# Attention and two gated layers on one core: the weights' conversion with a parametric ReLU on ACT and two DVE steps, and output weights in five fixed steps

## The chip, the core and the metric

The kernel runs on one core of a Trainium2 chip. Its engines work side by side: TensorE (PE) multiplies matrices, with its weight loads (PEld) beside it, VectorE (DVE), ScalarE (ACT) and GpSimd (POOL) do elementwise work, and SP issues transfers between HBM and the core's memory. The metric is the device time of one execution in microseconds; smaller is better. Three runs of the kernel before took 1116.43 to 1116.81 us, with a median of 1116.7 us.

## The reference, cut to what matters

```python
out1 = attention(q, k, v, mem_k, mem_v)      # 4 batches, 8 heads, 768 tokens in chunks of 32
x = out1 as (3072 tokens, 512)
x = ((x @ w1) * (x @ w2) @ w3) @ w_out       # moe:  512 -> 1024 -> 1024 -> 512, w3 @ w_out first
x = ((x @ w_a) * (x @ w_b)) @ w_out          # moe2: 512 -> 1536 -> 512
```

The weights (`moe_w1`, `moe_w2`, `moe_w3`, `moe_w_out`, `moe2_w_a`, `moe2_w_b`, `moe2_w_out`) come as 64-bit floating point numbers. [...]

## The kernel before

**Conversion of a block.** A block `raw` holds 512 or 1024 numbers per partition, each as a low word `l` and a high word `h`. `w_scale` (lines 372 to 379) runs on ACT: line 378 multiplies the high word, read as a 32-bit number, by a power of two, and line 379 does the like to the low word. `w_bits` (lines 381 to 385) runs on DVE: line 383 shifts the high word left by 3 and clears the sign bit, line 384 takes the sign bit out of `h` and sets it in the shifted word, and line 385 adds the low part. The names of the results are `w_f` (blocks of `w3` and the first `w_out`, 13 conversions) and `dec` (all others, 52).

**Stage 1, to about 95 us.** PE multiplies `w3` by `w_out` (`wps`), in two halves of 64 products. Between the products the attention of the first 14 or so units runs: scores `sc`, maximum `mx` (line 186 and 187), exponentials on ACT (line 209), the sum's reciprocal (lines 220 and 221), a multiplication on POOL (line 222), transposes `pt` and the product with the values `xp`. The order in which all this is issued is written out: `attn_slot` advances the attention by one slot, `w_tick` the conversions by one step. Four PSUM banks hold `wps`; `w_evict` empties them through ACT (line 570) and DVE (line 571), and the second half of the products takes the banks as they come free.

**Stage 2, to about 567 us.** For six tiles of 512 tokens `ab_step` forms `psA` and `psB` (w1 and w2), their product `gv` on DVE (line 635) with its two halves on ACT (636) and POOL (637), and `psY`. `between` stands after each half of a step and issues one `w_tick` while blocks of w1 and w2 remain, later one step of `c_weights` (the blocks of w_a and w_b), and the attention's slots for the next tile.

**Stage 3, to the end.** Three passes (`seq`) over pairs of token tiles; in each, twelve steps `f` of `seven`: 42 products `ps` in seven groups of six, with their sums on ACT (`copied`, line 830) and DVE (`plus`, line 835), and at the end `times` (lines 840 to 842 on DVE, ACT and POOL). Behind each step from the second on, 12 products `ops` with the output weights `fo` of the step before. In the first pass alone the output weights are converted as well: `w_out_blocks` is a generator with four steps for a block (scale on ACT; bits on DVE; upper half on ACT, line 143; lower half on DVE, line 146), and `other(n)` in `seven` runs `n` steps of it: two after the fifth group, one after the sixth, two at the end. With four steps for a block and five in a round of `seven`, the place of a block's step differs from round to round.

PE, DVE, ACT and POOL each work through their own queue in the order in which the program issues; an instruction that waits holds up all behind it on its engine.

Of the kernel before, what the change touches and what calls it, by code (L numbers as in the profile page):

```python
# [10 lines left out]
AF = mybir.ActivationFunctionType  # L11
ALU = mybir.AluOpType
# [31 lines left out]
def tile_attention_moe(  # L44
# [16 lines left out]
    nc = tc.nc  # L61
# [80 lines left out]
    def split_hi(hi, src):  # L142
        nc.scalar.activation(hi, src, AF.Copy)

    def split_lo(lo, src, hi):
        nc.vector.tensor_tensor(lo, src, hi.bitcast(F32), ALU.subtract)  # L146
# [225 lines left out]
    def w_scale(r):  # L372

        l, h = r[:, :, 0], r[:, :, 1].bitcast(F32)
        nc.scalar.activation(h, h, AF.Copy, scale=2.0**-112)  # L378
        nc.scalar.activation(l, l, AF.Copy, scale=2.0**-29)

    def w_bits(a, r):
        l, h = r[:, :, 0], r[:, :, 1]
        nc.vector.tensor_scalar(a, h, 3, 0x7FFFFFF8, ALU.logical_shift_left, ALU.bitwise_and)  # L383
        nc.vector.scalar_tensor_tensor(a, h, 0x80000000, a, ALU.bitwise_and, ALU.bitwise_or)  # L384
        nc.vector.tensor_tensor(a, a, l, ALU.add)  # L385

    def halves_of(i, *tiles):
# [52 lines left out]
    def w_new(pool, tag, n=None):  # L440
        return pool.tile([P, 2, CH], F32R, tag=tag, bufs=n, name=tag)
# [14 lines left out]
    def blocks_of(stage, src, out, bufs, raws_n=2):  # L456

        raws = []

        def load():  # L460
            if src:
                r = stage.tile([P, CH, 2], U32, tag="raw64", bufs=raws_n, name="raw64")
                nc.sync.dma_start(out=r.rearrange("p c w -> p (c w)"), in_=src.pop(0))
                raws.append(r)

        load()
        load()
        yield
        while raws:
            r = raws.pop(0)  # L470
            w_scale(r)
            yield
            a = stage.tile([P, CH], U32, tag="dec", bufs=bufs, name="dec")
            w_bits(a, r)
            load()
            out.append(a.bitcast(F32))
            yield
# [185 lines left out]
    def x_new():  # L663
        t = wpool.tile([P, 2, 2 * CH], F32R, tag="w12", name="x7")
        return t.rearrange("p l (k t) -> p l k t", k=2)
# [5 lines left out]
    def minus(x, y):  # L671
        z = tmp()
        nc.vector.tensor_tensor(z, x, y, ALU.subtract)
        return z

    def y_load(t, n):
        y = tmp()
        nc.sync.dma_start(out=y, in_=yd[t][:, n, :])
        return y

    def x_first(xs, k, t):
        b11, b21 = y_load(t, k), y_load(t, 2 + k)
        x_put(xs[0], k, b11)
        x_put(xs[1], k, b21)
        return b11, b21
# [12 lines left out]
    def w7_load(f):  # L698
        t = xpool.tile([P, 2, KD, TT], F32R, tag="xt", name="w7")
        t = t.rearrange("p l k t -> p (l k t)")[:, 0 : 7 * CH]  # L700
        src = wcd[f].rearrange("p i c -> p (i c)")
        for c0, c1 in ((0, 3 * CH), (3 * CH, 7 * CH)):
            nc.gpsimd.dma_start(out=t[:, c0:c1].bitcast(F32), in_=src[:, c0:c1])  # L703
        w7.append(t.rearrange("p (i l k f) -> p i l k f", i=7, l=2, k=2))

    w7 = []
# [87 lines left out]
    def w_out_blocks():  # L794
        blocks = []
        conv = blocks_of(stage2, [w2o[f] for f in range(M2)], blocks, 1)
        next(conv)
        yield
        for f in range(M2):
            for _ in range(2):  # L800
                next(conv)
                yield
            if f < 4:
                w = cp.tile([P, 2, CH], F32R, tag="fo", bufs=4, name="fo")
            else:
                w = w_new(wpool, "wo")
            x = blocks.pop()
            split_hi(w[:, 0, :], x)
            yield
            split_lo(w[:, 1, :], x, w[:, 0, :])  # L810
            fo.append(w)
            yield

    def product(ps, i, w, first):
        n = 0
        for k in range(2):
            for a, b in PASSES:
                nc.tensor.matmul(  # L818
                    ps,
                    lhsT=w[:, i, a, k, :],  # L820
                    rhs=xs[i][:, b, k, :],
                    start=first and n == 0,
                    stop=n == 5,
                    skip_group_check=not first,
                )
                n += 1

    def copied(ps):
        z = tmp()
        nc.scalar.activation(z, ps, AF.Copy)  # L830
        return z

    def plus(ps, y):
        z = tmp()
        nc.vector.tensor_tensor(z, ps, y, ALU.add)  # L835
        return z

    def times(x, y, g2):
        z = tmp()
        nc.vector.tensor_tensor(z, x, y, ALU.mult)  # L840
        nc.scalar.activation(g2[:, 0, :], z, AF.Copy)  # L841
        nc.gpsimd.tensor_tensor(g2[:, 1, :], z, g2[:, 0, :].bitcast(F32), ALU.subtract)  # L842

    def bank():
        return psd.tile([P, 512], F32, tag="d", name="ps7")[:, :TT]

    def seven(w, g1, g2, other, after):

        pa, pb = bank(), bank()
        product(pa, 0, w, True)  # L850
        s1 = copied(pa)
        next(late, None)
        product(pb, 1, w, True)
        c11 = plus(pb, s1)
        next(late, None)
        product(pa, 2, w, False)
        u2 = copied(pa)
        next(late, None)
        pc = bank()
        product(pc, 3, w, True)  # L860
        s5 = copied(pc)
        product(pa, 4, w, False)
        c22 = plus(pa, s5)
        other(2)
        product(pc, 5, w, False)
        c12 = plus(pc, u2)
        other(1)
        product(pa, 6, w, False)
        after()
        times(pa, c11, g1)  # L870
        times(c12, c22, g2)
        other(2)

    def out_part(ops, f, g2):
        for s in range(NS):
            for i, (a, b) in enumerate(PASSES):
                mm(
                    ops[s],
                    g2[:, a, P * s : P * s + P],
                    fo[f][:, b, :],  # L880
                    f == 0 and i == 0,
                    f == M2 - 1 and i == 2,
                )

    def out_new(pool, tag):
        return [pool.tile([P, 512], F32, tag=tag, name="ops") for _ in range(NS)]

    def out_store(ops, t):
        for s in range(NS):
            ob = tmp()  # L890
            if s % 2 == 0:
                nc.vector.tensor_copy(ob, ops[s])
            else:
                nc.scalar.activation(ob, ops[s], AF.Copy)
            r0 = t * TT + s * P
            nc.sync.dma_start(out=out[r0 : r0 + P, :], in_=ob)
# [6 lines left out]
    def other(n):  # L903
        for _ in range(n):
            next(cw, None)

    seq = [NT1 - 2] + list(range(0, NT1 - 2, 2))
    for si, t in enumerate(seq):
        nxt = seq[si + 1] if si + 1 < len(seq) else None
        g1, g2 = [], []  # L910
        spare = xs.pop().rearrange("p l k t -> p k l t")
        ops = out_new(pso, "o")
        for f in range(M2):
            g1.append(cp.tile([P, 2, TT], F32R, tag="g1", bufs=3, name="g1"))
            if f < M2 - 2:
                g2.append(cp.tile([P, 2, TT], F32R, tag="g2", bufs=M2 - 2, name="g2"))
            else:
                g2.append(spare[:, f - M2 + 2])

            def after():  # L920
                if f + 2 < M2 or nxt is not None:
                    w7_load((f + 2) % M2)

            seven(w7.pop(0), g1[f], g2[f], other, after)
            while len(fo) < f:
                next(cw)
            if f > 0:
                out_part(ops, f - 1, g1[f - 1])
        while len(fo) < M2:
            next(cw)  # L930
        ops2 = out_new(psd, "d")
        out_part(ops2, 0, g2[0])
        out_part(ops, M2 - 1, g1[M2 - 1])
        out_store(ops, t)
        if nxt is not None:
            xs = [x_new() for _ in range(8)]
            for k in range(2):
                b11, b21 = x_first(xs, k, nxt)
                b12, b22 = y_load(nxt + 1, k), y_load(nxt + 1, 2 + k)
                t1 = minus(b12, b11)  # L940
                x_put(xs[3], k, t1)
                for _ in x_rest(xs, k, b11, b21, b12, t1, b22):
                    pass
        for f in range(1, M2):
            out_part(ops2, f, g2[f])
        out_store(ops2, t + 1)
        if si == 0:
            stagestack.close()
# [83 lines left out]
```

## Time and profile before

| | |
|---|---|
| median of three runs | 1116.7 us |
| the profiled execution | 1116.64 us, span 1114.9 us |
| PE busy | 1094.1 us, 98% of the span |
| PEld busy | 874.9 us, 78% |
| DVE busy | 613.8 us, 55% |
| ACT busy | 516.3 us, 46% |
| POOL busy | 295.5 us, 27% |
| mean granted clock of TensorE | 0.998 |

The span runs from the first to the last instruction; 1.7 us of the execution lie outside it. PE is busy nearly throughout, so the time can only change where PE waits, or where its clock or the number of its instructions changes. The views that are read for that are the list of waits of PE, the groups by line, the order of time around each wait, and the busy time by stretches.

### The profile page before, as it was taken

To read this page: it belongs to the slowest core of one execution; us is meant where nothing else is said; L and a number is where in the kernel's file an instruction comes from. 1 tells how busy PE (TensorE), PEld (TensorE's weight loads), DVE (VectorE), ACT (ScalarE), POOL (GpSimd) and SP (SyncE) were. 2 spreads that over 40 slices of the span, in tenths; PEclk is the share of its full clock that TensorE was granted. 3 is DMA by queue.
4 is the path that set the end of the run, shared out by engine and by line. 5 is a ranking of instruction groups with operands and counts; after the bars stand their busy time and mean duration, and the time that the engine had idled before them with its cause. 6 is when DMAs were issued, how large, how long until landed. Compare 5 with 4: busy or idle time off the path is not lost.

```text
span 1114.9 us, 15510 instructions
## 1 busy us (share of the span) xinstructions
PE 1094.1 (98%) x5354; PEld 874.9 (78%) x5354; DVE 613.8 (55%) x1342; ACT 516.3 (46%) x1299; POOL 295.5 (27%) x308
## 2 busy tenths in 40 slices
PE   8899999999999999999999999999999999999998
PEld 3456888888878888888877878888888888888887
DVE  6879966876886777755766564252322243322220
ACT  6777656766766766745453343232222223222210
POOL 2452232321321322221212333202232211232210
PEclk9999999999999999999999999999999999999999
DMA  8845536345445444437545555424344352344311
GB/s 300 276 136 173 153 100 224 111 146 185 133 137 185 140 137 147 148 111 234 191 161 192 190 193 192 173 90 153 133 159 172 132 179 103 133 154 177 132 38 38
DMA packets 61671, 174.55 MB, mean 157 GB/s; under 512 B 8022, under 2 KB 18080, under 8 KB 55577
## 3 DMA queue, kind: packets, MB, share of 16 engines
q1 hardware_dynamic: 48762, 102.38, 27.7%
q0 software_dynamic: 12544, 70.91, 17.8%
q8 instruction: 42, 0.69, 0.3%
q14 instruction: 36, 0.29, 0.1%
q10 hardware_dynamic: 287, 0.27, 0.1%
HBM read 139.97 MB, written 33.55 MB: 156 GB/s over the span
## 4 chain that ended last, share of the span: by engine, by line
PE 85%; DVE 3%; ACT 2%; issue 1%; DMA 0%; DVEq 0%; ACTq 0%
PE ps L818 29%; PE ops L92 17%; PE psA L92 11%; PE psB L92 11%; PE psY L92 11%; PE sc L92 2%; PE xp L92 2%; PE pt L230 1%; DVE dec L384 1%; DVE dec L385 0%; ACT t L209 0%; DVE dec L383 0%; DMA wc<-co 0%; ACT raw L378 0%; DVE x L146 0%
## 5 line engine op out<-in xcount | busy, mean ns | idle before, releaser
L818 PE MATMUL ps<-x,w 128*128 128x512 f32 x1512 | 349.6, 390 | 3.8 <-ACT tmp L830 3.8
L818 PEld LDWEIGHTS ps<-x,w 128*128 128x128 f32 x1512 | 283.3, 188 | 64.7 <-ACT tmp L830 5.9
L835 DVE TENSOR_TENSOR tmp<-ps,tmp 128x512 f32<-128x512 f32 x108 | 74.6, 691 | 245.0 <-PE ps L818 240.9
L92 PE MATMUL psA<-xt,w 128*128 128x512 f32 x576 | 143.3, 398 | 0.0
L92 PE MATMUL psB<-xt,w 128*128 128x512 f32 x576 | 141.3, 394 | 0.0
L92 PE MATMUL psY<-g,wo 128*128 128x512 f32 x576 | 139.0, 393 | 0.0
L703 POOL DMA_DIRECT2D w<-wc x72 | 40.1, 559 | 368.9 <-PE ps L818 368.5
L830 ACT ACTIVATE tmp<-ps 128x512 f32<-128x512 f32 x108 | 64.6, 598 | 146.8 <-PE ps L818 133.9
L92 PEld LDWEIGHTS psA<-xt,w 128*128 128x128 f32 x576 | 106.8, 190 | 22.2 <-DVE dec L383 0.2
L92 PEld LDWEIGHTS psY<-g,wo 128*128 128x128 f32 x576 | 105.8, 188 | 21.3
L92 PEld LDWEIGHTS psB<-xt,w 128*128 128x128 f32 x576 | 105.5, 188 | 21.3
L222 POOL TENSOR_TENSOR t<-t,sm 96x512 f32<-96x512 f32 x64 | 67.7, 1058 | 196.3 <-DVE sm L221 107.9
L92 PE MATMUL ops<-wo,g 128*128 128x512 f32 x504 | 118.6, 389 | 0.0
L637 POOL TENSOR_TENSOR g<-gv,g 128x512 fp32r<-128x512 f32 x48 | 66.2, 1379 | 173.8 <-ACT g L636 173.6
L92 PEld LDWEIGHTS ops<-wo,g 128*128 128x128 f32 x504 | 94.6, 188 | 19.6
L841 ACT ACTIVATE g<-tmp 128x512 fp32r<-128x512 f32 x66 | 40.8, 635 | 130.4 <-DVE tmp L840 130.4
L842 POOL TENSOR_TENSOR g<-tmp,g 128x512 fp32r<-128x512 f32 x66 | 87.1, 1343 | 26.5 <-ACT g L841 26.0
L209 ACT ACTIVATE t<-t,mx 96x128 f32<-96x128 f32 x168 | 65.2, 393 | 7.8 <-DVE mx L194 7.8
L92 PE MATMUL ops<-fo,g 128*128 128x512 f32 x288 | 68.2, 389 | 0.0
L92 PE MATMUL wps<-w_f 128*128 128x512 f32 x128 | 59.7, 597 | 4.5 <-DVE w_f L385 2.6
L92 PEld LDWEIGHTS ops<-fo,g 128*128 128x128 f32 x288 | 54.1, 188 | 11.2
L636 ACT ACTIVATE g<-gv 128x512 fp32r<-128x512 f32 x48 | 30.3, 631 | 51.6 <-DVE gv L635 50.8
(83 smaller groups left out, 1293.7 us busy)
## 6 DMA issues: line engine op xcount, KB each, us to landing
w<-wc POOLq DMA_DIRECT2D x36, 1024.0 KB, 6.8
w<-wc POOLq DMA_DIRECT2D x36, 768.0 KB, 4.9
wc<-co SPq DMA_DIRECT2D x84, 256.0 KB, 2.5
raw<-in_wab SPq DMA_DIRECT2D x24, 512.0 KB, 4.0
kraw<-in_kt SPq DMA_DIRECT2D x42, 256.0 KB, 3.1
raw<-in_w SPq DMA_DIRECT2D x16, 512.0 KB, 3.8
raw<-in_w3a SPq DMA_DIRECT2D x7, 1024.0 KB, 9.0
vraw<-in_vw SPq DMA_DIRECT2D x50, 128.0 KB, 3.3
```

What stands on the lines that cost most here:

```text
L92: nc.tensor.matmul(o, lhsT=l, rhs=r, start=first, stop=last)
L209: nc.scalar.activation(t[:, h, :], src[:, h, :], AF.Exp, bias=mx[:, h : h + 1], scale=scale, accum_out=sm[:, h : h + 1],)
L222: nc.gpsimd.tensor_tensor(t, t, sm[:, :, None].to_broadcast([GQ, HH, KW]), ALU.mult)
L230: nc.tensor.transpose(pt[:, h, :], t[:, h, :], id_sb)
L636: nc.scalar.activation(g2[:, 0, :], gv, AF.Copy)
L637: nc.gpsimd.tensor_tensor(g2[:, 1, :], gv, g2[:, 0, :].bitcast(F32), ALU.subtract)
L703: nc.gpsimd.dma_start(out=t[:, c0:c1].bitcast(F32), in_=src[:, c0:c1])
L818: nc.tensor.matmul(ps, lhsT=w[:, i, a, k, :], rhs=xs[i][:, b, k, :], start=first and n == 0, stop=n == 5, skip_group_check=not first,)
L830: nc.scalar.activation(z, ps, AF.Copy)
L835: nc.vector.tensor_tensor(z, ps, y, ALU.add)
L841: nc.scalar.activation(g2[:, 0, :], z, AF.Copy)
L842: nc.gpsimd.tensor_tensor(g2[:, 1, :], z, g2[:, 0, :].bitcast(F32), ALU.subtract)
```

## The change

`w_scale` scales the high word with a parametric ReLU in place of a copy: positive numbers are multiplied by 2^-112 as before, negative ones by 2^-112 and by 2^32, which sets one more bit in the exponent field. `w_bits` shifts the word left by 3 with nothing cleared: the sign is shifted out, and that bit of the exponent comes to stand where the sign belongs. Line 384 is gone, and the low part is added as before.

`w_out_blocks` has a fifth step for each block, in which nothing is issued, so that a block takes exactly one round of `seven`. The two steps at the end of a round are moved ahead, to behind the sum of the second group, and are left out in the round f = 0.

```diff
         l, h = r[:, :, 0], r[:, :, 1].bitcast(F32)
-        nc.scalar.activation(h, h, AF.Copy, scale=2.0**-112)
+        nc.scalar.activation(h, h, AF.Prelu, scale=2.0**-112, alpha=2.0**32)
         nc.scalar.activation(l, l, AF.Copy, scale=2.0**-29)
 
     def w_bits(a, r):
         l, h = r[:, :, 0], r[:, :, 1]
-        nc.vector.tensor_scalar(a, h, 3, 0x7FFFFFF8, ALU.logical_shift_left, ALU.bitwise_and)
-        nc.vector.scalar_tensor_tensor(a, h, 0x80000000, a, ALU.bitwise_and, ALU.bitwise_or)
+        nc.vector.tensor_scalar(a, h, 3, None, ALU.logical_shift_left)
         nc.vector.tensor_tensor(a, a, l, ALU.add)
...
             for _ in range(2):
                 next(conv)
                 yield
+            yield
...
-    def seven(w, g1, g2, other, after):
+    def seven(w, g1, g2, other, after, lead):
...
         c11 = plus(pb, s1)
         next(late, None)
+        other(lead)
         product(pa, 2, w, False)
...
         times(c12, c22, g2)
-        other(2)
...
-            seven(w7.pop(0), g1[f], g2[f], other, after)
+            seven(w7.pop(0), g1[f], g2[f], other, after, 2 * (f > 0))
```

The order of PE, POOL and SP is the same in both kernels. DVE has 65 instructions fewer; ACT has the same number, in another order in the first pass of stage 3.

On DVE, at the conversion of a w1/w2 block early in stage 2 (`dec` is the block, `mx` the maximum of the scores, `gv` the product that the next matmuls are waiting for), before:

```order
L383 TENSOR_SCALAR dec<-raw_796 128x512
L384 SCALAR_TENSOR_TENSOR dec<-raw_796,dec 128x512
L385 ISA dec<-raw_796,dec 128x1024
L186 TENSOR_REDUCE mx<-sc 96x4
L187 TENSOR_SCALAR mx<-mx 96x4
L635 TENSOR_TENSOR gv<-psB,av 128x512
```

and after:

```order
L383 TENSOR_SCALAR dec<-raw_778 128x512
L384 ISA dec<-raw_778,dec 128x1024
L186 TENSOR_REDUCE mx<-sc 96x4
L187 TENSOR_SCALAR mx<-mx 96x4
L634 TENSOR_TENSOR gv<-psB,av 128x512
```

Between the shift and the add one instruction is gone, and `mx` and `gv` move up by one place; the same holds wherever a block is converted.

On ACT, in the first pass of stage 3, from the end of one round of `seven` into the next (L378 and L379 scale a block, L841 makes the upper halves of the round's two products, L143 `wo<-dec` is the upper half of a block of output weights, L830 copies a group's sum out of PSUM), before:

```order
L378 ACTIVATE raw_6525<-raw_6525 128x512
L379 ACTIVATE raw_6525<-raw_6525 128x512
L841 ACTIVATE g_6575<-tmp 128x512
L841 ACTIVATE g_6576<-tmp 128x512
L143 ACTIVATE wo<-dec 128x512
L830 ACTIVATE tmp<-ps_6672 128x512 x2
L830 ACTIVATE tmp<-ps_6698 128x512
```

and after:

```order
L378 ACTIVATE raw_6455<-raw_6455 128x512
L379 ACTIVATE raw_6455<-raw_6455 128x512
L841 ACTIVATE g_6586<-tmp 128x512
L841 ACTIVATE g_6587<-tmp 128x512
L830 ACTIVATE tmp<-ps_6680 128x512
L143 ACTIVATE wo<-dec 128x512
L830 ACTIVATE tmp<-ps_6680 128x512
L830 ACTIVATE tmp<-ps_6709 128x512
```

The upper half of a block now stands behind the first copy of a round in place of ahead of it, and it belongs to the block whose bits were made in the round before.

## Rows read from the trace of the kernel before

**Rows 1.** The page's first part: busy time, share of span, instructions.
```profile
PE 1094.1 (98%) x5354; PEld 874.9 (78%) x5354; DVE 613.8 (55%) x1342; ACT 516.3 (46%) x1299; POOL 295.5 (27%) x308
```

**Rows 2.** Waits of PE: who, for whom: us in total, times, longest us.
```profile
PE ps L818 <- ACT tmp L830: 3.8, 4, 1.5
PE wps L92 <- DVE w_f L385: 2.6, 2, 1.4
PE xp L92 <- ACT p L234: 2.2, 1, 2.2
PE wps L92 <- DVE wo L571: 1.9, 1, 1.9
PE sc L92 <- DVE mx L187: 1.8, 1, 1.8
...
PE sc L92 <- DVE q L146: 1.6, 2, 1.1
PE pt L230 <- ACT p L234: 0.6, 1, 0.6
PE sc L92 <- DVE w_f L383: 0.5, 1, 0.5
```

**Rows 3.** Groups by line, shapes apart: busy us, mean ns, idle before.
```profile
L384 DVE SCALAR_TENSOR_TENSOR dec<-raw,dec 128x512 uint32<-128x512 uint32 x52 | 45.8, 880 | 1.8
L209 ACT ACTIVATE t<-sc,mx 96x128 f32<-96x128 f32 x88 | 30.8, 360 | 17.4 <-DVE mx L187 17.3
L384 DVE SCALAR_TENSOR_TENSOR w_f<-raw,w_f 128x1024 uint32<-128x1024 uint32 x11 | 14.2, 1291 | 0.4
L378 ACT ACTIVATE raw<-raw 128x1024 f32<-128x1024 f32 x11 | 12.8, 1161 | 4.8 <-DMA raw<-in_w3a 4.8
L143 ACT ACTIVATE xt<-xp 128x128 fp32r<-128x128 f32 x4 | 1.1, 275 | 0.5 <-PE xp L92 0.3
```

**Rows 4.** Order of time, second `w3` block: start us, us, instruction [idle before].
```profile
11.76 1.15 ACT L379 ACTIVATE raw<-raw 128x1024 uint32<-128x1024 uint32 x1
12.62 1.23 DVE L384 SCALAR_TENSOR_TENSOR w_f<-raw,w_f 128x1024 uint32<-128x1024 uint32 x1
13.98 1.23 DVE L385 CUSTOM_DVE_ANT_0 w_f<-raw,w_f 128x2048 uint16<-128x2048 uint16 x1
```

**Rows 5.** Order of time, one attention unit in stage 1.
```profile
25.70 1.04 PE L92 MATMUL sc<-kraw,qraw 67*96 67x128 f32 x8
27.09 0.68 DVE L383 TENSOR_SCALAR w_f<-raw 128x1024 uint32<-128x1024 uint32 x1
31.80 0.68 DVE L383 TENSOR_SCALAR w_f<-raw 128x1024 uint32<-128x1024 uint32 x1
31.99 1.09 PE L92 MATMUL sc<-kraw,qraw 67*96 67x128 f32 x8 [1.81 <-DVE mx L187]
```

**Rows 6.** Order of time, ahead of the banks' change between halves.
```profile
51.84 1.23 DVE L384 SCALAR_TENSOR_TENSOR w_f<-raw,w_f 128x1024 uint32<-128x1024 uint32 x1
```

**Rows 7.** Order of time on DVE; then a stretch's busy time, PEclk, DMA share, GB/s.
```profile
102.24 0.69 DVE L384 SCALAR_TENSOR_TENSOR dec<-raw,dec 128x512 uint32<-128x512 uint32 x1
104.77 0.69 DVE L635 TENSOR_TENSOR gv<-psB,av 128x512 f32<-128x512 f32 x1 [0.21 <-issue]
...
100.00:120.00 20.00, 17.79 (x93) 14.31 (x92) 18.50 (x32) 13.95 (x38) 5.91 (x5) 0.91 0.48 149
```

**Rows 8.** Order of time around 317 us: POOL and DVE.
```profile
317.16 1.31 POOL L637 TENSOR_TENSOR g<-gv,g 128x512 fp32r<-128x512 f32 x1
317.37 1.66 DVE L384 SCALAR_TENSOR_TENSOR dec<-raw,dec 128x512 uint32<-128x512 uint32 x1
```

**Rows 9.** Order of time, first pass of stage 3, around 655 us.
```profile
652.36 3.15 DVE L384 SCALAR_TENSOR_TENSOR dec<-raw,dec 128x512 uint32<-128x512 uint32 x1
656.38 0.63 ACT L143 ACTIVATE wo<-dec 128x512 fp32r<-128x512 f32 x1 [3.74 <-DVE dec L385]
```

**Rows 10.** Groups by line: the load of ACT's table.
```profile
L378 ACT ACT_TABLE_LOAD x1 | 1.3, 1283 | 3.1 <-issue 3.1
```

## The prediction
> **What bounds the kernel now.** I began with the busy times of the engines [rows 1]: PE works 1094.1 of 1114.9 us, DVE 55% and ACT 46%. Nothing taken off DVE can shorten the kernel except through the 20.8 us in which PE stands still, and through its clock. So the second view is the list of PE's waits [rows 2], where the reader is to see two things: the eight rows shown add to 15.0 us, and every one of them ends on DVE or ACT, none on a transfer or POOL. The other 5.8 us are PE's start, the stores at the end and a remnant of 0.2 us; nothing in the change reaches those. The third view is the order of time ahead of each wait, to see whether a conversion step stands in the queue that PE waits for. The groups by line [rows 3] then give what the removed step costs.
>
> **The change, part by part.** The removed step, line 384, takes 52 x 0.880 us + 11 x 1.291 us = 60.0 us of DVE [rows 3] (two small ones more at the very start). It lies beside a busy PE nearly everywhere, where its removal is worth nothing; what it is worth is what follows, wait by wait.
>
> How much of one step comes back is itself a choice. At 317 us the step takes 1.66 us, and it ends 0.6 us after a POOL multiplication that began just ahead of it [rows 8]; undisturbed it takes 0.69 us [rows 7]. So the mean of 0.880 us has time in it in which DVE is held up by POOL, and the add of line 385, which now follows the shift at once, may inherit that hold. I count 0.69 us plus the 0.1 us between two instructions for a 512 block, 1.23 + 0.13 us for a 1024 block [rows 4], and leave the hold out. The Trainium skill, GPSIMD Engine Reference, section 1 (Specifications), says that GpSimd and VectorE share their interfaces to SBUF, and that it is DVE instructions with two SBUF inputs, or in a two-port mode, that contend; the add has two such inputs, so by that rule the hold moves to it, and the DVE time saved would be nearer 50 than 60 us. Rows 8 agree with it for line 384; no row shows the add alone behind a shift.
>
> *Start.* PE's second block of `w3` waits for line 385 (1.4 of the 2.6 us, [rows 2]). The add began at 13.98 us, behind line 384 at 12.62. Without that step it still needs the low word's scaling, which ends at 11.76 + 1.15 = 12.91 us [rows 4], so it begins at about 13.0: **1.0 us** sooner. Bounds: 0.7 (the scaling slips) to 1.36 (13.98 - 12.62).
>
> *Attention units in stage 1.* DVE repeats a unit's work every 31.80 - 27.09 = 4.71 us [rows 5]. PE's own work between two scores is 31.99 - 25.70 - 1.81 = 4.48 us. DVE is the slower of the two, by little; without 1.36 us its round is 3.35 us, and PE is the slower one by 1.1 us. The waits that come of it are 1.8, 0.6 and 0.5 us [rows 2], 2.9 in all. ACT is next late: its round is four exponentials of 0.36 us and two scalings of 1.16 us [rows 3], 3.8 us, with about half a microsecond for a copy or an eviction. That is close under 4.48, so I take **2.5 us**; bounds 1.5 (the first wait shrinks by half a step only, since transfers also lie on that loop) and 2.9.
>
> *Change of banks.* The second half's products wait 1.9 us for line 571 [rows 2], and a line 384 of 1.23 us is issued ahead of it on DVE [rows 6]. Taking 1.23 + 0.13 off gives **1.3 us**; bounds 1.2 and 1.9.
>
> *The wait at 110 us.* `xp` waits 2.2 us for an ACT copy [rows 2]; ACT had itself been waiting for `gv`, which DVE reached at 104.77 us, with one line 384 of 0.69 us at 102.24 in front and two more since 95 us [rows 7]. If DVE is behind all that time, three steps of 0.8 us come back, 2.4 us, more than the wait; if only the last counts, 0.8. After this pause the clock fell: the stretch from 100 to 120 us has a mean granted clock of 0.91 [rows 7], which at the two levels of 2.4 and 1.2 GHz is 3.6 us at the lower one, and 20 x 0.09 = 1.8 us of lost work. So the place is worth between 0.8 us (a shorter pause, and the clock falls all the same) and 4.0. The orders show no other work in front of `gv`, so I take nearly all, **3.7 us**.
>
> *The waits around 322 and 337 us.* Together 1.6 us, for the attention's `q` on DVE [rows 2], behind a line 384 of 1.66 us [rows 8]. I take **1.1 us**, the longer of the two, and leave the other (0.5) standing; bounds 0.7 and 1.6.
>
> *The first pass of stage 3.* Four waits of PE for ACT's copy, 3.8 us [rows 2]. One of them in full: line 384 on DVE runs from 652.36 to 655.51; ACT's upper half `wo` waits 3.74 us for the block and starts at 656.38 [rows 9]; the copy that PE waits for stands behind it in ACT's queue. The five fixed steps undo exactly this: the first copy of a round stands ahead of the upper half now, and the upper half belongs to a block made a round earlier, so it waits for nothing. What it is moved past: on ACT it now stands ahead of the second copy, where 0.63 us fit between the first copy and the end of the third group; on DVE the lower half stands ahead of no wait. The bits stand before the sum of the sixth group, as before, without the removed step. Three of the four waits go, **3.4 us**; the fourth, 0.3 us in the round f = 0, has no block's step in front. Bounds 2.7 and 3.8.
>
> *ACT's parametric ReLU.* The trace has none. From below: no gain, the instruction moves the same 512 or 1024 numbers. From above by the nearest rows: an exponential on 128 columns takes 0.360 us, a copy on 128 columns 0.275 [rows 3], so another function with its operands costs 0.085 us at most for each of 65. The changed instruction has constants for all its operands, as the copy has, so I take zero; 0.085 us fits in ACT's slack.
>
> The sum is 1.0 + 2.5 + 1.3 + 3.7 + 1.1 + 3.4 = 13.0 us off the profiled execution's 1116.64 us. That one lies within 0.1 us of the median of the runs, so **1103.6 us**. All lower bounds together give 7.7 us less (1109), all upper bounds 15.6 us less (1101).
>
> **The rivals.** *Only the last stage gains.* DVE's relief in the first 340 us is passed on: ACT, 0.7 us under PE's pace in a unit, and the transfers become the next late ones there, and the pause at 110 us remains with its clock. Then 1.0 + 3.4 us and about 1 us of the rest come: 1111. For it speaks that ACT is just under PE's pace; against it, that PE's waits there end on DVE by name.
>
> *The removed waits come back elsewhere.* DVE's adds inherit POOL's hold, and PE, being earlier, meets transfers: the gain is eaten up, 1114.5 to 1118.9. Against it: the order of stage 3 is fixed and its gain depends on no hold.
>
> *ACT becomes the bound (the other side).* If the parametric ReLU cost two passes, 1.16 us more for a 1024 block, ACT's round in stage 1 would be 3.8 + 0.5 + 1.2 = 5.5 us against PE's 4.48: 1 us late in each of 11 blocks, and some 0.3 us in each of the 16 blocks of w1 and w2, against 3.4 us won in stage 3: 1116.7 + 11 + 5 - 3.4 = 1129. It decides from about 0.2 us more for a block on. Against it: the exponential is an ordinary function at 0.085 us over a copy.
>
> *The table is reloaded.* Were the parametric ReLU in another table than the exponential, a load of 1.283 us [rows 10] would stand at each of the 72 changes between the two that the changed kernel's order has on ACT, on an engine with little slack: 72 x about 1 us, some 1185 us. The changed program has one load, before the first scaling, as before, so I give it one chance in a hundred. The Trainium skill, ScalarE: Activation LUTs, section Table sets: the hidden batching unit, makes this its rule, to group functions by table set, and speaks of 2.7 us for a switch; by that figure it would be 72 x 2.7 = 194 us. Rows 10 agree on the load alone.
>
> **How the numbers follow.** The forecast (1101 to 1109) has 0.70; still faster than that, 0.06; only the last stage 0.12; eaten up 0.07, of which 0.06 lie within 0.2% and 0.01 above; ACT as the bound 0.04; the table 0.01. 0.2%, 2.2 us, is about what a measurement of this kernel can tell from no change. So faster 0.88, same 0.06, slower 0.06. The range from 1101 to 1112 leaves out the 0.06 below, 0.03 of the case in which only the last stage gains, and the three last, 0.12: 0.21 in all.
>
> **What would show it.** Right: line 384's group is gone from DVE, which is busy 50 to 60 us less; ACT's busy time is the same to 1 us, and line 378 still takes 1.16 us for 1024; the waits of PE for `mx`, `wo` and `p` in the first 120 us are together under 2.5 us; the stretch from 95 to 120 us has a granted clock of 1.00; the waits of `ps` are a single one of 0.3 us. Wrong: a line 378 of more than 1.3 us; an add of line 385 whose mean is up by as much as line 384 took; a wait of PE for a transfer; another stretch with a clock under 1.

## The result, and the profile after

The kernel after takes **1105.28 us** (median of four runs, 1102.74 to 1107.22) against 1116.76 of the kernel before beside it: a ratio of 0.9894, with a 95% interval of 0.9872 to 0.9916. The prediction was 1103.6 us in a range of 1101 to 1112. The profiled execution took 1104.78 us, its span 1103.0, 11.9 us less than the span before.

The busy times on the page, to be held against [rows 1]:

```profile
PE 1092.9 (99%) x5354; PEld 874.8 (79%) x5354; DVE 548.5 (50%) x1277; ACT 514.8 (47%) x1299; POOL 294.0 (27%) x308
```

DVE is busy 65.3 us less, ACT 1.5 us less, PE with the same instructions 1.2 us less. The waits of PE (who, for whom: us in total, times, longest), against [rows 2]:

```profile
PE sc L92 <- DVE sm L220: 1.7, 1, 1.7
PE warm L92 <- DVE wz L551: 1.6, 1, 1.6
PE wps L92 <- DVE w_f L384: 1.1, 2, 0.8
PE sc L92 <- DVE q L146: 0.9, 2, 0.5
PE xp L92 <- ACT p L234: 0.4, 1, 0.4
PE ps L818 <- ACT tmp L830: 0.3, 1, 0.3
```

Without `warm`, which is PE's start and was there before, 4.4 us are left of 15.0. Two things in this list lead through all that follows: the wait of 1.7 us of the scores is nearly as long as the one before it (1.8), and its place has a lower clock now. The order of time on PE at that place (start us, us, instruction, idle before it):

```profile
13.97 1.98 PE L92 MATMUL wps<-w_f 128*128 128x512 f32 x4 [0.85 <-DVE w_f L384]
...
30.62 1.09 PE L92 MATMUL sc<-kraw,qraw 67*96 67x128 f32 x8 [1.74 <-DVE sm L220]
31.54 3.58 PE L92 MATMUL wps<-w_f 128*128 128x512 f32 x4
```

Four products of `wps` take 1.88 us elsewhere in this trace and 3.58 here: behind the pause PE works at about half its clock. The stretches (busy time of PE, PEld, DVE, ACT and POOL, then PEclk, DMA share, GB/s) show it too, of after:

```profile
20.00:40.00 20.00, 18.27 (x70) 9.82 (x69) 13.21 (x26) 16.24 (x43) 10.89 (x16) 0.91 1.02 341
...
100.00:120.00 20.00, 19.60 (x116) 16.16 (x115) 17.29 (x33) 17.43 (x50) 6.86 (x6) 1.00 0.62 191
```

and of before, in the first of the two (the second is in [rows 7]):

```profile
20.00:40.00 20.00, 17.72 (x68) 9.24 (x66) 18.52 (x28) 16.26 (x42) 8.71 (x13) 1.00 0.86 312
```

The low clock at 110 us is gone, and a new one stands at 31 us. Two columns point at what the prediction did not see: DVE's busy time fell from 18.52 to 13.21 us, and the DMA engines went from a share of 0.86 to 1.02. The faster conversion asks for its next blocks sooner (the first one of `in_w3b` is issued at 27.00 us, before at 30.42), and in this stretch the DMA engines have no room left for that. The last experiments test it.

Where the 11.9 us come from is read by setting the starts of the same instruction in both traces side by side:

| place, instruction on PE | before | after | gained so far | gained here |
|---|---|---|---|---|
| second block of `w3`, `wps` | 15.26 | 13.97 | 1.29 | 1.29 |
| scores ahead of the banks' change | 50.57 | 49.68 | 0.89 | -0.40 |
| `xp` behind the banks' change | 57.15 | 54.09 | 3.06 | 2.17 |
| first `psA` | 95.30 | 91.78 | 3.52 | 0.46 |
| `psB` behind the wait for the `p` copy | 116.88 | 109.94 | 6.94 | 3.42 |
| `sc` behind the first wait for `q` | 322.65 | 314.94 | 7.71 | 0.77 |
| `ps` at the head of stage 3 | 574.24 | 566.62 | 7.62 | -0.09 |
| last `ops` of the first pass | 713.45 | 701.53 | 11.92 | 4.30 |

### The profile page after: what moved, and what is told of

The parts are those of the page before. It is cut to its first block, busy times and chain, and to the rows that moved or that the text cites. A ratio compares the mean times of both kernels' runs of the same rounds, so it can differ in the third digit from the quotient of the medians.

```text
span 1103.0 us, 15442 instructions
## 1 busy us (share of the span) xinstructions
PE 1092.9 (99%) x5354; PEld 874.8 (79%) x5354; DVE 548.5 (50%) x1277; ACT 514.8 (47%) x1299; POOL 294.0 (27%) x308
## 4 chain that ended last, share of the span: by engine, by line
PE 92%; DVE 3%; DMA 2%; ACT 2%; issue 1%; SPq 0%; DVEq 0%; ACTq 0%
PE ps L818 31%; PE ops L92 18%; PE psA L92 12%; PE psB L92 11%; PE psY L92 11%; PE sc L92 3%; PE wps L92 3%; PE xp L92 2%; PE pt L230 2%; DMA raw<-in_w3a 1%; ACT t L209 1%; DMA raw<-in_w 0%; ACT raw L379 0%; ACT raw L378 0%; DVE w_f L384 0%
## 5 line engine op out<-in xcount | busy, mean ns | idle before, releaser
L830 ACT ACTIVATE tmp<-ps 128x512 f32<-128x512 f32 x108 | 64.6, 599 | 157.8 <-PE ps L818 140.9
L841 ACT ACTIVATE g<-tmp 128x512 fp32r<-128x512 f32 x66 | 40.7, 633 | 139.8 <-DVE tmp L840 139.8
L842 POOL TENSOR_TENSOR g<-tmp,g 128x512 fp32r<-128x512 f32 x66 | 84.1, 1294 | 20.2 <-ACT g L841 19.4
```

## The experiments

Twelve runs were made, the kernel after itself among them. Each stands beside runs of the kernel before on the same chip; these had medians of 1117.65 us (the first four kernels), 1116.66 (the next four), 1116.70 (the two `e9`) and 1117.73 (the two `e10`), so that differences of less than 1 us between kernels of different groups say nothing.

**The two halves of the change, each alone.** First the kernel after once more, as the measure for the rest:

> The changed kernel once more, beside the experiments. Theory: its remaining pause of 1.74 us before the scores at 30.6 us, and the 1.7 us lost to the lower clock behind it, come in most executions but not in all, so the runs lie between 1102.5 and 1107.5 us, and a run whose granted clock is 1.000 is the fastest. Rival: the spread has another source, and runs with a clock of 1.000 are as slow as the others.

Measured: 1104.86 us (1102.38 to 1107.89), ratio 0.9892 [0.9874, 0.9909]. The theory failed in both parts: two of the five runs lie outside its range, by 0.1 and 0.4 us, and the run with a clock of 1.000 took 1104.86 us while the fastest, 1102.38, had 0.999; so the clock alone does not order the runs, as the rival has it. The spread of 5.5 us is large beside what is to be explained. Two executions of this kernel were profiled, of 1104.78 and 1102.38 us, and of the 2.40 us between them 2.32 lie ahead of the first `psA` (91.78 and 89.46 us), that is, in stage 1: in the faster one the scores wait 1.16 us in place of 1.74, and no low clock follows.

Then the parametric ReLU and the two DVE steps in the old order, that is, the kernel before with

```diff
-        nc.scalar.activation(h, h, AF.Copy, scale=2.0**-112)
+        nc.scalar.activation(h, h, AF.Prelu, scale=2.0**-112, alpha=2.0**32)
...
-        nc.vector.tensor_scalar(a, h, 3, 0x7FFFFFF8, ALU.logical_shift_left, ALU.bitwise_and)
-        nc.vector.scalar_tensor_tensor(a, h, 0x80000000, a, ALU.bitwise_and, ALU.bitwise_or)
+        nc.vector.tensor_scalar(a, h, 3, None, ALU.logical_shift_left)
```

> The parametric ReLU and the two DVE steps alone, output weights in the old order. Theory (the order is worth what the three waits for ACT's copy cost, 3.4 to 4 us): 1109 us, with three waits of PE for the copy of line 830. Rival (the waits came from the length of line 384, so the missing step ends them by itself): 1105 to 1106 us, and these waits together are under 1 us.

and the new order with the old copy and three DVE steps, the same lines undone in the kernel after:

> The five fixed steps alone, conversion with the copy and three DVE steps as before. Theory: 1112.7 to 1113.3 us, the waits for line 830 down to one of 0.3 us, all earlier waits as before. Rival (the DVE step is what counts in the last stage too): 1115 to 1117 us.

Measured: 1107.45 us (0.9902 [0.9887, 0.9918]) with the bits alone, 1113.25 us (0.9956 [0.9943, 0.9970]) with the order alone. Three rows from the list of waits of the first:

```profile
PE sc L92 <- ACT raw L378: 2.6, 2, 2.3
...
PE ps L817 <- ACT tmp L829: 1.9, 3, 0.9
...
PE xp L92 <- ACT p L234: 0.4, 1, 0.4
```

and of the second:

```profile
PE xp L92 <- ACT p L234: 2.2, 1, 2.2
...
PE wps L92 <- DVE wo L571: 1.9, 1, 1.9
PE sc L92 <- DVE mx L187: 1.7, 1, 1.7
...
PE ps L819 <- ACT tmp L831: 0.3, 1, 0.3
```

So the two halves work at different places: the bits alone clear `xp` and the banks' change and take `ps` from 3.8 to 1.9 us; the order alone takes `ps` to 0.3 and leaves the early waits about as they were. From the `ps` at the head of stage 3 to the last `ops` of the first pass (the last two rows of the table) the traces have 139.21 us before, 137.00 with the bits, 135.04 with the order and 134.91 with both. So the order is worth 4.17 us on the kernel before and 2.09 once the bits are done (the medians say 4.4 and 2.6), and the bits alone bring 2.21: half of stage 3's gain is to be had either way. The first result lies between the 1109 of the theory and the 1105 to 1106 of the rival; the second is what its theory has.

**What the parametric ReLU costs.** The kernel after with a copy in its place:

```diff
-        nc.scalar.activation(h, h, AF.Prelu, scale=2.0**-112, alpha=2.0**32)
+        nc.scalar.activation(h, h, AF.Copy, scale=2.0**-112)
```

> The kernel after, with a plain copy that scales by 2**-112 in place of the parametric ReLU (it leaves the sign of negative weights out, so its output is not the reference's). Theory (the parametric ReLU costs what the copy costs): line 378 takes 0.66 us for 512 and 1.16 us for 1024 numbers, as after, ACT's busy time is within 1 us of 514.8 us, and the time within 1102.5 to 1107.5 us. Rival (the ReLU has a price that the mean hides): line 378 is shorter by up to 0.085 us, ACT's busy time by up to 5 us.

Line 378 (groups by line: busy us, mean ns, idle before) in after:

```profile
L378 ACT ACTIVATE raw<-raw 128x512 f32<-128x512 f32 x54 | 35.9, 664 | 1.9 <-DMA raw<-in_w3a 1.8
...
L378 ACT ACTIVATE raw<-raw 128x1024 f32<-128x1024 f32 x11 | 12.7, 1155 | 4.6 <-DMA raw<-in_w3a 3.4 <-DVE w_f L384 1.3
L378 ACT ACT_TABLE_LOAD x1 | 1.3, 1283 | 3.1 <-issue 3.1
```

and with the copy:

```profile
L378 ACT ACTIVATE raw<-raw 128x512 f32<-128x512 f32 x54 | 35.9, 665 | 1.8 <-DMA raw<-in_w3a 1.8
...
L378 ACT ACTIVATE raw<-raw 128x1024 f32<-128x1024 f32 x11 | 12.7, 1152 | 4.3 <-DMA raw<-in_w3a 4.3
```

664 against 665 ns, 1155 against 1152: it costs what the copy costs. Its single time, 1104.80 us, is that of after. The table is loaded once. In this trace the wait of the scores at 30.7 us, the same program place that the list of after puts down to `sm`, has another releaser:

```profile
PE sc L92 <- DMA qraw<-in_qt: 1.8, 1, 1.8
```

**What the wait at 110 us was made of.** The old step for the sign was put back into the kernel after for single blocks: for the one whose line 384 stood at 102.24 us before [rows 7], and for this and the two blocks ahead of it, at 95.03 and 98.74 us (17 <= i <= 19 in the last line).

```diff
-    def w_bits(a, r):
+    def w_bits(a, r, keep=False):
...
         nc.vector.tensor_scalar(a, h, 3, None, ALU.logical_shift_left)
+        if keep:
+            nc.vector.scalar_tensor_tensor(a, h, 0x80000000, a, ALU.bitwise_and, ALU.bitwise_or)
         nc.vector.tensor_tensor(a, a, l, ALU.add)
...
-            w_bits(a, r)
+            w_bits(a, r, i == 19)
```

> The kernel after, with the old OR of the sign kept in one block alone, the last one whose conversion stands ahead of gv at 100 to 105 us (at 102.24 us before). Theory (the steps ahead of gv add up, 0.8 us each): the wait of PE for the p copy near 107 us goes from 0.4 to about 1.2 us; 1105 to 1106 us. Rival (only the last step counts and the two before it are absorbed): the whole wait of before comes back, about 2.2 us, and with it the clock of 0.91 between 100 and 120 us: 1108 to 1109 us.

> The same with the old OR kept in three blocks, those whose steps stood at 95.03, 98.74 and 102.24 us before. Theory (they add up): the wait near 107 us is about 2.2 to 2.8 us, the clock between 100 and 120 us is 0.91 again, and the time is 3.7 us over after, about 1109 us. Rival (only the last counts): the same as with one block. Second rival (the wait of before was made further up, by the lateness that DVE carries from the attention units): the wait stays at 0.4 to 0.8 us with either, and the time at 1105.

Measured: 1105.91 us (1105.08 to 1111.21; 0.9908 [0.9882, 0.9934]) with one step, 1109.29 us (1108.41 to 1112.39; 0.9934 [0.9914, 0.9953]) with three. The wait is 0.4 us with none. On PE with one step:

```profile
107.75 0.55 PE L92 MATMUL xp<-p,vraw 128*64 128x96 f32 x8 [1.09 <-ACT p L234]
108.23 3.02 PE L92 MATMUL psA<-xt,w 128*128 128x512 f32 x12
```

and with three:

```profile
109.80 0.55 PE L92 MATMUL xp<-p,vraw 128*64 128x96 f32 x8 [2.20 <-ACT p L234]
110.28 4.61 PE L92 MATMUL psA<-xt,w 128*128 128x512 f32 x12
```

One step adds 0.69 us, its own length; three add 1.80, 0.60 each, and give the wait of before to 0.01 us, and with it the clock: the twelve products take 4.61 us, as they did in before, and 3.02 with one step. From the scores ahead of the wait to `psB` behind it pass 5.53 us in after (104.41 to 109.94), 8.93 with three steps (106.08 to 115.01), 8.94 before (107.94 to 116.88). Three instructions of 0.7 us off the path of PE's wait are worth 3.4 us, of which the clock is 1.6. (The total of the kernel with three steps holds something else too: waits of 2.2 and 1.3 us for the scores in stage 1, with a clock of 0.91 from 40 to 60 us.)

**What is left in stage 1: DVE's rounds or a transfer?** In after POOL issues `k` and `q` of unit 3 at 25.71 and 26.24 us, and PE takes up their scores at 30.62; in before these are 27.88, 28.40 and 31.99 us. That one transfer of `q` (KB, us from issue to landing), in before:

```profile
qraw<-in_qt POOLq DMA_DIRECT2D x1, 96.0 KB, 3.5
```

and in after:

```profile
qraw<-in_qt POOLq DMA_DIRECT2D x1, 96.0 KB, 4.2
```

So `q` lands at 31.9 and at 30.4 us, 0.1 and 0.2 us ahead of the scores, in both kernels. The scores need `k`, `q` and one of two buffers in PSUM, and that buffer was free since the exponentials of unit 1 (over at 28.8 us before, at 26.9 after); `mx` and `sm`, which the lists name, only ended at about the same time. Measured from the scores of unit 2 (25.70 us before, 24.41 after), `q` was issued 0.87 us sooner in after and took 0.7 longer to land, so the pause went from 1.81 to 1.74 us and no further.

The first test gave unit 3 buffers of its own, so that its `k` and `q` are loaded right behind those of unit 2:

```diff
-    qbuf = [att.tile([P, HH, GQ], F32, tag=f"q{i}", bufs=1, name="qraw") for i in range(2)]
+    qbuf = [(p0 if i == 2 else att).tile([P, HH, GQ], F32, tag=f"qb{i}", bufs=1, name="qraw") for i in range(3)]
...
+    def slot_of(u):
+        return 2 if u == 3 else u % 2
...
+                if s // 3 + 2 == 3:
+                    a_mask(5, queue_of(5))
...
+                    if s // 3 + 2 == 2:
+                        a_load(3)
```

> The changed kernel with a buffer of its own for k and q of the fourth attention unit, loaded right behind the third unit's in place of some 8 us later. Theory (the pause before the scores at 30.6 us is for the landing of that unit's k and q, not for DVE, which the list of waits names): the pause is gone, the clock stays at 1.00 there, and the time is 1101 to 1102 us. Rival (PE waits for DVE there): the pause stays at 1.5 us or more and the time is as that of the changed kernel, 1105 us.

Measured: **1102.44 us** (1101.72 to 1103.02; 0.9862 [0.9847, 0.9876]), 2.4 us under after on the same chip and below the medians of both kernels; the theory's 1101 to 1102 was missed by 0.4. The pause at unit 3 is gone, as the theory has it, but unit 4 has one:

```profile
29.25 0.81 POOL L126 DMA_DIRECT2D kraw<-in_kt  x1
30.05 0.53 POOL L127 DMA_DIRECT2D qraw<-in_qt  x1
```

```profile
35.49 1.08 PE L92 MATMUL sc<-kraw,qraw 67*96 67x128 f32 x8 [1.80 <-DVE sm L223]
```

Unit 4 still loads late (first fence, on POOL) and waits as long as unit 3 did (second, on PE). The clock stays at 1.00 here, though the pause is no shorter, so most of what this kernel saves is the low clock. The next test gave two units a buffer of their own, so that units 3 to 6 load one unit earlier (against after, in part):

```diff
+    def slot_of(u):
+        return u - 1 if u in (3, 4) else u % 2
...
+                u = s // 3 + 2
+                if 3 <= u <= 5:
+                    a_load(u + 1)
+                elif u <= NPLAIN + 1 and u != 6:
+                    a_load(u)
+                    if u == 2:
+                        a_load(3)
```

> The kernel after, with two more pairs of buffers for the plain k and q, so that units 3 to 6 are loaded one unit earlier than after (units 2 and 3 behind each other, then 4, 5, 6; 7 as before). Theory (what is left of the pause in stage 1 is the landing of a unit's own k and q, and with one more buffer it only went on to the next unit): no wait of the scores in stage 1 over 0.5 us, clock 1.00 from 20 to 60 us, 1100.3 to 1101 us. Rival (the waits end on DVE, whose rounds are late): a wait of about 1.7 us stays at unit 3 or 4 and the time at 1102.4. Second rival (the DMA engines are full there, so earlier loads of k and q delay the weights' blocks): the wait goes over to the wps products, 1102 to 1104.

Measured: 1103.58 us (1103.08 to 1104.63; 0.9881 [0.9864, 0.9897]). The theory's 1100.3 to 1101 was missed. No wait of the scores over 0.5 us is left in stage 1, as it has it, but now PE stands still, at 37.6 us, for a transpose that waits for ACT:

```profile
PE pt L233 <- ACT p L237: 1.2, 1, 1.2
```

Two kernels took the same end without a buffer, by issuing the loads on POOL ahead of the multiplication that it waits for, for two units and, with 11 in place of 2, for all:

```diff
+            early = s % 3 == 0 and 1 <= s // 3 <= 2
             for _, u, stage_of in sorted(todo.get(s, []), key=lambda x: x[:2]):
-                stage_of(u)
+                if not (early and stage_of is a_norm):
+                    stage_of(u)
+            if early:
+                a_load(s // 3 + 2)
+                a_norm(s // 3 - 1)
...
-                if s // 3 + 2 <= NPLAIN + 1:
+                if s // 3 + 2 <= NPLAIN + 1 and not 1 <= s // 3 <= 2:
```

> The kernel after, in which POOL issues the loads of k and q of units 3 and 4 right behind the scores that free their buffers, ahead of the multiplication with the sum of the unit before (no further buffer). In the trace of after, POOL stood idle ahead of that multiplication from about 20 us on, while the scores of unit 1 were over at 21.1 us and the loads were issued at 24.9 to 26.8. Theory (what is left of the pause is the landing of these loads): issued some 3.5 us sooner at unit 3 and 3 us sooner at unit 4, they land before PE wants them; no wait of the scores over 0.5 us, clock 1.00 from 20 to 60 us, about 1100 us, below the 1102.4 of the third buffer. Rival (DVE's rounds are late, the landing is a coincidence): a wait of 1.2 to 1.8 us stays, 1102 to 1105 us. Second rival (the DMA engines are full from 20 to 40 us): the wait goes over to the weights' blocks, as with two more buffers, 1102 to 1104.

> The same order for all of the loads of k and q that POOL issues (units 3 to 13). Theory: as with two, 1100 us, since only units 3 and 4 wait for a landing; the later units have 1 us or more to spare. Rival (a load that waits for the scores holds POOL's multiplication up, and with it PE's transposes): new waits of PE for p or t in 40 to 70 us, 1101 to 1104 us.

Measured: 1103.23 us (0.9875 [0.9858, 0.9891]) and 1103.35 us (0.9882 [0.9867, 0.9896]). The theory's 1100 was missed again, and the pause went on again. With two loads moved, no wait of the scores is left in stage 1, and PE stands still for a transpose instead (with all of them moved the same transpose waits 1.33 us, at 37.83):

```profile
38.98 0.52 PE L230 MATMUL pt<-id_sb,t 96*128 96x96 f32 x4 [2.26 <-ACT p L234]
```

It waits for ACT's copy `p`, which starts at 38.36 us behind two scalings, and these had waited for a block of weights. It was the third block in a row that came late to ACT (0.26, 0.72 and 0.76 us), where in after ACT waits for none from 20 to 36 us. ACT's order of time (the scalings are lines 383 and 384 in this kernel):

```profile
36.35 1.13 ACT L383 ACTIVATE raw<-raw 128x1024 f32<-128x1024 f32 x1 [0.76 <-DMA raw<-in_w3b]
37.38 1.09 ACT L384 ACTIVATE raw<-raw 128x1024 uint32<-128x1024 uint32 x1
38.36 0.47 ACT L234 ACTIVATE p<-pt 128x384 f32<-128x384 f32 x1
```

The second rival of the two loads is right: the wait goes over to the weights. The DMA issues say why (KB each, median us from issue to landing, 15 to 40 us). In after:

```profile
raw<-in_w3b SPq DMA_DIRECT2D x3, 1024.0 KB, 7.2
kraw<-in_kt POOLq DMA_DIRECT2D x5, 128.0 KB, 5.0
```

and with the two loads moved:

```profile
raw<-in_w3b SPq DMA_DIRECT2D x3, 1024.0 KB, 9.4
kraw<-in_kt POOLq DMA_DIRECT2D x4, 128.0 KB, 6.2
```

In before these were 5.1 and 4.3 us. In this stretch what is issued sooner lands later, `k` and weights alike.

The last two kernels take the transfers away. In the first, `k` and `q` of units 3 to 6 are not loaded, in the second `v` of units 2 to 6 isn't either (the last three lines; `vfirst` keeps the tiles of units 0 and 1):

```diff
-        a_qk(u, queue_of(u))
+        if not 3 <= u <= 6:
+            a_qk(u, queue_of(u))
...
+        if 2 <= u <= 6:
+            vraw[u] = vfirst[u % 2]
+            return
```

> The kernel after, in which k and q of units 3 to 6 are not loaded; the units compute on what their buffers hold, so the output is not the reference's. No wait for a landing of k or q is left in 20 to 45 us, and 4 x 224 KB less are moved there, 2.6 us at the 341 GB/s of after. Theory (the pauses of stage 1 that are left are transfers', first the landing of k and q, then the weights' blocks behind a full set of DMA engines): no wait of PE over 0.5 us from 20 to 45 us, clock 1.00, the DMA share of 20 to 40 us under 1, and 1099.5 to 1101 us. Rival (DVE's or ACT's rounds are what is late there): a wait of 1 us or more stays between 20 and 45 us with a releaser on DVE or ACT that itself had waited for no transfer; 1102 to 1104 us.

> As before it, and v of units 2 to 6 is not loaded either (those of units 0 and 1 stand in for them, the output is not the reference's): 5 x 128 KB less, 1.9 us more at 341 GB/s. Theory (the DMA engines are full): the weights' blocks land sooner again, ACT's waits for them between 20 and 45 us shrink, and the time falls by another 0 to 1 us, 1099 to 1100.5 us; not more, since PE's remaining waits there are then under 0.5 us. Rival (only the landing of k and q counts, not the filling of the engines): the same as without k and q, to 0.3 us, and ACT's waits for blocks as long as there.

Measured: 1100.89 us (1100.76 to 1101.04; 0.9850 [0.9834, 0.9867]) and 1100.96 us (1100.71 to 1101.24; 0.9851 [0.9836, 0.9865]). Without `k` and `q` the list of PE's waits has nothing left from 20 to 45 us, and the stretch shows PE working through it at full clock, with the DMA engines below their full share:

```profile
PE wps L92 <- DVE w_f L385: 1.7, 2, 0.9
PE warm L92 <- DVE wz L552: 1.6, 1, 1.6
PE sc L92 <- DVE q L147: 0.8, 2, 0.5
PE xp L92 <- ACT p L235: 0.4, 1, 0.4
PE ps L819 <- ACT tmp L831: 0.3, 1, 0.3
```

```profile
20.00:40.00 20.00, 20.00 (x84) 11.35 (x83) 14.76 (x30) 19.30 (x54) 8.26 (x10) 1.00 0.89 322
```

DVE and ACT do the same work as in after, and are not late for anything. Dropping `v` too changes nothing, as its rival has it, since no wait is left for it to shorten; whether `v` alone would have helped is left open by that. So the transfers cost after 1104.86 - 1100.89 = 4.0 us, about 1.7 in the pause, 1.7 in the clock behind it (3.58 - 1.88 us), the rest within what the groups of runs differ by. The traces agree: of 3.94 us between the profiled executions of after and of the kernel without `k` and `q`, 3.83 lie ahead of the first `psA` (91.78 and 87.95 us). The spread is smaller as well: the two kernels without `k` and `q` have four runs each within 0.3 and 0.5 us, after has 5.5. That landings alone make the spread is not shown: the third buffer's kernel, with a pause of 1.80 us, has 1.3.

## Why the prediction was right, and where it was off

The time came 1.7 us above the forecast, inside its range. Of the 13.0 us forecast for the profiled execution, 11.9 came. The mechanism, a wait of PE behind a step that the change takes away or moves, held at five of the six places. That the sum came so near is in part luck: the sixth place fell 2.4 us short, and the change of banks, the first pass and the start gave 2.1 us more than forecast. (All lower bounds together are 7.6 us, not 7.7; the 1109 that follows is the same.) Step by step, against the table of places:

- **Start**, 1.0 predicted, bounds 0.7 and 1.36: 1.29 us. The add begins as the low word's scaling ends, at 12.69 us, as predicted. The 0.3 us more is luck: the block itself came earlier, its high word is scaled from 10.47 us on, before from 10.71. In the other trace of after that is 10.72, and the gain is 1.04 us.
- **Attention units in stage 1**, 2.5 predicted: this is the step that failed. Up to the change of banks the units lost 0.40 us; with the 0.46 won behind it they gave 0.06. The waits of 0.6 and 0.5 us went, the wait of 1.8 became one of 1.74, and behind it came a low clock that took 1.7 us. The prediction read "every one of them ends on DVE or ACT, none on a transfer" from the list, and took the name on a wait for its cause. `mx` (before), `sm` (after) and the DMA of `q` (with the copy) are named for one and the same pause: whichever ended last beside it. The runs showed the landing of `q` in its place, 3.5 us behind its issue before and 4.2 after; with `k` and `q` away the pause is gone. What would have told is the trace of before: POOL's queue, where `k` and `q` of unit 3 stand behind the multiplication and the mask, the landing of `q` 0.1 us ahead of the scores, and the DMA share of 0.86. The rival by which only the last stage gains has the transfers become the next late ones, and was right in that for this one term alone. It was wrong of ACT, whose scalings of two blocks start 3.44 us apart in after (19.83, 23.27, 26.71, 30.15 us), not 3.8 + 0.5: no copy and no eviction stands in these rounds, two scalings of 1.14 to 1.17 us start 1.03 to 1.05 us apart, and four exponentials take 1.37, since neighbouring instructions on ACT overlap. The Trainium skill, ScalarE: Activation LUTs, section What ACT_TABLE_LOAD costs, gives about 93 ns for this overlap; the trace, with 0.11 to 0.15 us between the scalings of these rounds, is near it. The prediction had added durations up without it.
- **Change of banks**, 1.3 predicted, bounds 1.2 and 1.9: the whole wait went, 2.17 us from start to start. More than one step's length was to be had: against the scores ahead of the change (50.57 us before, 49.68 after) the shift ahead of the last line 571 already starts 1.09 us sooner (51.12, 49.14), and from there to line 571 DVE gains the other 1.25 (54.53, 51.30), the step itself.
- **The wait at 110 us**, 3.7 predicted: 3.42. Of the two readings in the prediction, that three steps add up or that only the last counts, the experiment decides for the first, and the low clock behind the pause of 2.2 us is 1.6 of the 3.4.
- **The waits for `q`**, 1.1 predicted, bounds 0.7 and 1.6: 0.68. The longer one went from 1.10 to 0.35, the other stayed (0.49, now 0.52), as said.
- **First pass of stage 3**, 3.4 predicted, bounds 2.7 and 3.8: 4.30 us, above the bounds. The mechanism is as described, one wait of 0.3 us is left, but the list counts idle time from the modelled end of the last matmul, and each wait costs 0.2 to 0.3 us more from start to start. The same shows at the banks' change, where a listed wait of 1.9 us was worth 2.17. The order alone gave 4.17 us in its trace.
- **The parametric ReLU**, zero predicted: 664 and 1155 ns, as the copy. Both rivals that hung on it fall. The Trainium skill, ScalarE: Activation LUTs, section Table sets: the hidden batching unit, warns of a load wherever the next function is in another table set. Here the program has one load of 1283 ns, as in [rows 10], though the two functions alternate.

**The hold of DVE by POOL.** DVE saved 65.3 us; the prediction expected 50 to 60. The removed group was 60.0 us, and two small instructions of it 0.7 each. The add did not inherit what the group lost but became shorter, from 979 to 793 ns over 52 `dec` blocks, 9.7 us; other instructions became longer by 5.8 us in sum, most of all `cs` of line 508 and `sm` of line 220 (3.8 and 3.5 us). What decides is the order of the starts. In before POOL's subtraction for the lower half of `gv` (line 637, which the prediction calls a multiplication) begins first, and the add 0.45 us behind it (start us, us):

```profile
156.72 1.46 POOL L637 TENSOR_TENSOR g<-gv,g 128x512 fp32r<-128x512 f32 x1 [2.48 <-ACT g L636]
157.17 1.55 DVE L385 CUSTOM_DVE_ANT_0 dec<-raw,dec 128x1024 uint16<-128x1024 uint16 x1
```

In after the add, with no step of line 384 ahead of it, begins first:

```profile
149.46 0.69 DVE L384 CUSTOM_DVE_ANT_0 dec<-raw,dec 128x1024 uint16<-128x1024 uint16 x1
149.74 1.55 POOL L636 TENSOR_TENSOR g<-gv,g 128x512 fp32r<-128x512 f32 x1 [3.08 <-ACT g L635]
```

So it is throughout: of the 52 adds on `dec`, 17 were long before (1.55 to 1.65 us) and 6 after (1.41 to 1.82), and each of these began behind a POOL instruction with two inputs (a subtraction or a multiplication) that was still at work. All others took 0.69 to 0.70 us, also the 17 of after that began 0.09 to 0.43 us ahead of one. The Trainium skill, GPSIMD Engine Reference, section 1 (Specifications), has such contention for DVE instructions with two SBUF inputs; the trace agrees for these 23 adds. The prediction had the rule and not the places: the hold moved to the add in six blocks of 52. Whether any part of the total hangs on it no run tested.

Of the signs that were listed, those for "right" held (line 384's group gone, line 378 the same, clock 1.00 from 95 to 120 us, a single `ps` wait of 0.3, the named waits under 2.5 us), but DVE was busy 65.3 us less where 50 to 60 were named, and ACT 1.5 us less where 1 was allowed. Of those for "wrong", two came, both at 31 us: a wait for a transfer and another stretch with a clock under 1. The 4.0 us that the transfers cost are more than the 1.7 us by which the forecast was too low.

## What to carry to other kernels

A wait in the list has a length and a name, and the name can be that of an instruction that only ended at the same time: before a removed step is credited with the wait, look at all that the waiting instruction needs, loads and the queue that issues them included, and at the DMA share of the stretch. In this kernel an engine got faster in a stretch whose DMA engines were near full; its blocks were asked for sooner, and a better place for one load was paid for by another. Fewer bytes helped (4.0 us), another order of the same bytes less (2.4 us at most). Instructions ahead of a wait in one queue can add up, as three steps did at 110 us, and a wait cut short may give back the clock behind it as well.

## What the runs showed of the hardware

- The clock fell behind some pauses of PE and not behind others of the same length: behind 1.74 us (after), 1.79 (with the copy) and 1.93 us (one step) it did, behind 1.81 us (before), 1.74 (order alone) and 1.80 us (third buffer), all in 30 to 36 us, it did not. At the change of banks it fell behind 1.94 us (order alone; the next four products took 3.05 us) and not behind 1.91 (before; 1.98 us). Behind each of the six pauses of 2.16 to 2.28 us (before, bits alone, order alone, three steps with two, two loads moved) it fell, behind 1.09 at 107 us (one step) it did not. The length of the pause alone doesn't decide; no run here tells what does.
- A block of 1024 KB landed 5.1 us after its issue in before, 7.2 in after, 9.4 with two loads moved and 5.5 us without `k` and `q`, at DMA shares of 0.86, 1.02, 1.03 and 0.89 from 20 to 40 us: between 7.2 and 9.4 us the share hardly changes, and the landing time still tells the stretches apart.
- A DVE add with two inputs that began behind a running POOL instruction with two inputs took 1.41 to 1.82 us, one that began ahead of it 0.69, as long as alone.
- Runs of the kernel after spread by 5.5 us, those without `k` and `q` by 0.3, the third buffer's by 1.3, though PE still waits for a landing there.
